# Low parts of later weights by an accumulating load, and a reordered end, in a gated mix of an S4D convolution and a bilinear unit

## The chip, the cores and the metric

The kernel runs on one core of a Trainium2 chip. The metric is the device time of one execution in microseconds. A profile of one execution gives the span from its first to its last instruction and what each engine did: PE (TensorE, matmuls), DVE (VectorE), ACT (ScalarE), POOL (GpSimd) and SP (SyncE, which here only issues DMAs).

## The reference

```python
# u: (1, 2048, 512), N = 128, F = 1792
def _A_ref(u, ...):
    ...
    P = jnp.exp((A * dt[:, None])[:, :, None] * pos[None, None, :])
    K = 2.0 * jnp.einsum("dn,dnl->dl", C, P).real
    ...                                        # y = causal convolution of u with K, by FFT of length 2L
    return y + u * D_skip[None, None, :]

def _B_ref(x, w_gate, w_up, w_down):
    g = jnp.einsum("bsd,df->bsf", x, w_gate)
    u = jnp.einsum("bsd,df->bsf", x, w_up)
    h = g * u
    return jnp.einsum("bsf,fd->bsd", h, w_down)

g = _sigmoid((x * gate_w).sum(-1, keepdims=True))
return g * a + (1 - g) * b                     # a = _A_ref(x, ...), b = _B_ref(x, ...)
```

## The kernel before

**Two computations share the engines.** The bilinear unit is made of dense matmuls. The hidden columns F are 14 tiles of 128, taken in four groups, `GROUPS` = 0 to 2, 3 to 5, 6 to 9 and 10 to 13. For each group the four chunks of 512 tokens are walked, forwards and backwards in turn. For each tile f of the group `hidden` makes two products, pg (gate) and pu (up), 12 matmuls each; ScalarE copies pg out of its bank into h, VectorE multiplies it by pu. pg and pu have one buffer each, so the next pg waits for that copy. `down` then multiplies the group's h with the down weights into y, and `evacuate` scales y by one minus the gate into acc, which GpSimd adds to the output in HBM with an accumulating DMA. For the last group and the last chunk (`LAST` = 0) the rows are kept and added by `ends`.

**High and low parts.** Each operand is held as two numbers of the matmul's format: a high part (the rounded value) and a low part (what the rounding left). A product is three matmuls: high by low, low by high, high by high. The names are whi and wlo (gate and up weights, 1024 columns, halves c = 0 and 1), dhi and dlo (down weights, 512), xs (tokens), hh and hl (h). `weights` and `down_weights` load a weight tile by SP into raw (two buffers) and call `split`, which makes the high part by a ScalarE cast and the low part by a VectorE subtraction:

```python
add("act", 0.62, lambda: act.copy(at(hi, s), src()), r=[got], w=[ph], rank=0)
add(
    "dve", 0.69,
    lambda: dve.tensor_tensor(out=at(lo, z), in0=src(), in1=at(hi, s).bitcast(F32), op=ALU.subtract),
    r=[got, ph], w=[pl], rank=0,
)
```

A low part of gate and up is thus two subtractions, each on its half. `SLOTS` = 4 buffers hold the parts of a group; the next group's weights are made while the last chunk of the old group is worked on. This is called a change of groups below; there are three.

**The convolution** runs beside it on whatever time is left. `u_part` transforms the input (stored as su_d). Sixteen blocks of channels go through `phases`, `amplitudes`, `direct_powers`, `x_table` and `v_table`, which are long chains on ScalarE (exponentials and sines, with table loads between, squares) and VectorE (tiles t, rt, e, ri, su, di, m, x, v), to `k_block`, small matmuls k<-v,x. Four blocks are one quarter q of the channels, transformed in `k_first` (stored as sk_d). `transforms(q)` then makes the product in the frequency domain, T = 0 to 3 (`m_load`, `m_second`, `m_product`), goes back in `m_inverse` (stored as y_d) and in `m_last`, which multiplies by the gate and adds to the output by accumulating DMAs. In the last two quarters the 4 rows of each partition that belong to `ends` are kept (`late["fin"]`); `ends` loads those rows of the output into sums (traced as kt), adds the two kept pieces and acc, and stores them by SP (out<-kt).

**What sets the order.** Nothing above is issued as written. Each step is a task with an engine, a duration in microseconds, what it reads and writes, and a rank. `Work.run` plans all tasks by these numbers and then issues them; `InOrder` keeps each engine to the planned order. So a duration in the text moves instructions, and a change of one task can move any of the others. On the chip each engine takes its queue in order and waits at each instruction for what it needs. Traces show all instructions under line 119, that of `InOrder`; tiles tell them apart.

Of the kernel before, what the change touches and what calls it, by code (L numbers as in the profile page):

```python
# [319 lines left out]
def gated_mix_kernel(  # L320
# [33 lines left out]
    m_su, m_sk, m_y, m_out, m_xs = (work.memory() for _ in range(5))  # L354
# [111 lines left out]
    def weights(fs):  # L466
        for f in fs:
# [113 lines left out]
    def ends():  # L581
# [5 lines left out]
            w=[sums, *((m_out, t0 + r) for r in range(4))], dma=1024, rows=range(t0, t0 + 4),  # L587
        )
        for r, acc in ending:
            t = t0 + r  # L590
            for q, (fin, parts) in late["fin"].items():
                add(
                    "dve", 0.25,
                    lambda r=r, q=q, fin=fin: dve.tensor_tensor(
                        out=sums.t[:, r, P * q : P * q + P], in0=sums.t[:, r, P * q : P * q + P],
                        in1=fin.t[:, 4 * (LAST % 2) + r], op=ALU.add,
                    ),
                    r=parts, w=[(sums, (r, q))], rank=0,
# [47 lines left out]
    def u_part(t):  # L646
# [4 lines left out]
        def score_of(j):  # L651
# [3 lines left out]
                "dve", 0.77,  # L655
# [191 lines left out]
    def phases(b):  # L847
# [3 lines left out]
        tt(0.83, lambda: t.t, lambda: per_power(rates()[:, 1]), lambda: per_channel(turns), ALU.mult, [par, m_powers], [t])  # L851
        add("act", 0.77, lambda: act.activation(rt.t, t.t, AF.Identity, bias=shift[:, 0:1]), r=[t, m_const], w=[rt])

        add(
            "dve", 0.83,
# [6 lines left out]
            "act", 2.13 if b % 2 or not b else 0.83, lambda: act.activation(t.t, t.t, AF.Sin, scale=-TWO_PI), w=[t],  # L862
        )
        add(
            "act", 0.83, lambda: act.activation(rt.t, rt.t, AF.Sin, scale=-TWO_PI, bias=half_pi[:, 0:1]), r=[m_const],
# [6 lines left out]
    def direct_powers(b):  # L872
# [4 lines left out]
        for c in range(2):  # L877
            f = t if c else rt
            tt(0.83, lambda c=c: ri.t[:, c], lambda f=f: f.t, ampl, ALU.mult, [f, e], [(ri, c)])
# [72 lines left out]
    def v_table(b):  # L952
# [8 lines left out]
        add("act", 1.28, copies, r=[ri], w=[(v, 2)])  # L961
# [5 lines left out]
        for to, of, n in (((33, 64, 2), (0, 16, 1), 16), ((34, 64, 4), (33, 49, 2), 8)):  # L967
# [11 lines left out]
            us = 0.04 * n + 0.08  # L979
            add("act", 1.15 if n == 16 else 0.73, sq_act, r=src_parts, w=[(v, ("r", k)), sq])  # L980
# [15 lines left out]
    def k_block(b, x, v):  # L996
# [18 lines left out]
        add("act", 0.4, lambda: act.copy(side(1), pv(0)[:, :, :, ::-1]), r=[pk], w=[(kt, (1, b % 4))])  # L1015
# [398 lines left out]
```

## Time and profile before

| | |
|---|---|
| median of 3 runs | 606.57 us (606.55 to 610.38) |
| profiled execution | 608.69 us, span 606.9 us, granted clock 0.989 |
| PE busy | 586.3 us, 97% |
| DVE busy | 527.0 us, 87% |
| ACT busy | 389.8 us, 64% |
| POOL busy | 113.9 us, 19% |
| DMA moved | 129.73 MB, mean 214 GB/s |

The span leaves out what lies before the first and behind the last instruction. Matmuls overlap one another in the pipeline, so the busy time of PE is near the span even where it runs smoothly; what it loses is read from the starts of its instructions. A row of the timeline gives start, duration, engine, operation, output and inputs, and in brackets how long the engine was idle before it and who released it.

### The profile page before, as it was taken

What the parts mean: (1) busy time and instruction counts of PE and PEld (TensorE: products, weight loads), DVE (VectorE), ACT (ScalarE), POOL (GpSimd) and SP (SyncE); (2) the same over time, 40 slices, a digit from 0 to 9 for tenths busy, and PEclk for the clock granted to TensorE, in tenths of its full rate; (3) what the DMA queues carried; (4) which work ended last, traced back from release to release, by engine and by line L of the source; (5) the groups of instructions that cost most, each with busy time, mean ns of one, the idle gap of its engine ahead of it and who ended that gap; (6) DMA issues with size and microseconds to landing.
All of it is one profiled execution on the core that took longest, in us unless ns stands there. A gap on an engine that the chain in (4) does not pass through costs nothing.

```text
span 606.9 us, 15872 instructions
## 1 busy us (share of the span) xinstructions
PE 586.3 (97%) x6500; PEld 444.8 (73%) x6500; DVE 527.0 (87%) x841; ACT 389.8 (64%) x879; POOL 113.9 (19%) x173
## 2 busy tenths in 40 slices
PE   8889999999999999999999999999899999999993
PEld 5657676787877777786687877866688777777772
DVE  6999999999999999999799999979999950775725
ACT  5279688686679588758958665966877423434621
POOL 0011212300201340201324101003424021402101
PEclk9989999999999999999999999999899999999997
DMA  8899978575647796749989827886989269989876
GB/s 278 313 354 341 360 263 326 161 218 162 136 151 206 211 226 192 161 135 283 237 178 228 185 81 192 198 228 178 204 171 234 63 170 343 207 257 232 214 155 121
DMA packets 69276, 129.73 MB, mean 214 GB/s; under 512 B 6868, under 2 KB 35540, under 8 KB 66772
## 3 DMA queue, kind: packets, MB, share of 16 engines
q1 hardware_dynamic: 47476, 88.21, 45.8%
q0 software_dynamic: 21312, 40.38, 33.1%
q8 instruction: 51, 0.84, 0.6%
q14 instruction: 21, 0.17, 0.1%
q10 hardware_dynamic: 416, 0.13, 0.1%
HBM read 73.65 MB, written 55.05 MB: 212 GB/s over the span
## 4 chain that ended last, share of the span: by engine, by line
PE 67%; DVE 16%; DMA 10%; issue 4%; ACT 2%; POOLq 0%; SPq 0%; ACTq 0%; DVEq 0%; POOL 0%
PE pg L119 19%; PE pu L119 18%; PE y L119 17%; PE k L119 13%; DMA raw<-in_wts 5%; DVE v L119 3%; DVE x L119 2%; DMA y_d<-e 2%; DMA dt_d<-small 2%; DVE wlo L119 1%; DVE y L119 1%; DVE ri L119 1%; DVE t L119 1%; DVE m L119 1%; DMA x<-dt_d 1%
## 5 line engine op out<-in xcount | busy, mean ns | idle before, releaser
L119 PE MATMUL pg<-xs,whi 128*128 128x512 f32 x448 | 140.1, 394 | 0.5 <-ACT whi L119 0.4
L119 PE MATMUL pu<-xs,whi 128*128 128x512 f32 x448 | 138.2, 390 | 0.0
L119 PEld LDWEIGHTS pg<-xs,whi 128*128 128x128 f32 x448 | 85.0, 190 | 19.8 <-ACT whi L119 1.9
L119 PEld LDWEIGHTS pu<-xs,whi 128*128 128x128 f32 x448 | 84.1, 188 | 17.0
L119 PE MATMUL pg<-xs,wlo 128*128 128x512 f32 x224 | 90.2, 403 | 4.3 <-ACT h L119 3.8
L119 PE MATMUL y<-dhi,hl 128*128 128x512 f32 x224 | 91.1, 407 | 2.9 <-ACT acc L119 1.8
L119 PE MATMUL y<-dlo,hh 128*128 128x512 f32 x224 | 88.2, 394 | 1.6 <-DVE dlo L119 1.6
L119 PE MATMUL pu<-xs,wlo 128*128 128x512 f32 x224 | 89.6, 400 | 0.0
L119 PE MATMUL y<-dhi,hh 128*128 128x512 f32 x224 | 87.9, 393 | 0.0
L119 POOL DMA_DIRECT2D out<-acc x44 | 38.7, 918 | 243.3 <-ACT acc L119 204.7
L119 ACT COPY ev<-k 128x512 f32<-128x512 f32 x112 | 59.2, 594 | 17.2 <-PE k L119 17.2
L119 ACT CAST hh<-h 128x512 fp32r<-128x512 f32 x56 | 34.8, 621 | 44.6 <-DVE h L119 44.4
L119 PEld LDWEIGHTS y<-dhi,hl 128*128 128x128 f32 x224 | 42.4, 189 | 24.3 <-issue 7.8
L119 ACT ACTIVATE acc<-y,ngate 128x512 f32<-128x512 f32 x63 | 42.7, 688 | 25.6 <-PE y L119 20.6
L119 PEld LDWEIGHTS pg<-xs,wlo 128*128 128x128 f32 x224 | 42.5, 190 | 21.5 <-ACT h L119 6.8
L119 PEld LDWEIGHTS pu<-xs,wlo 128*128 128x128 f32 x224 | 42.0, 188 | 15.7 <-issue 7.0
L119 ACT COPY h<-pg 128x512 f32<-128x512 f32 x56 | 32.9, 587 | 31.5 <-PE pg L119 26.1
L119 DVE TENSOR_TENSOR h<-pu,h 128x512 f32<-128x512 f32 x56 | 38.6, 689 | 16.6 <-PE pu L119 15.4
L119 PEld LDWEIGHTS y<-dlo,hh 128*128 128x128 f32 x224 | 42.4, 189 | 9.8 <-DVE dlo L119 1.9
L119 PEld LDWEIGHTS y<-dhi,hh 128*128 128x128 f32 x224 | 42.5, 190 | 9.2
L119 DVE TENSOR_TENSOR hl<-h,hh 128x512 fp32r<-128x512 f32 x56 | 38.5, 688 | 3.7 <-ACT hh L119 3.4
L119 POOL DMA_DIRECT2D su_d<-ev x32 | 17.4, 550 | 96.4 <-ACT ev L119 96.4
(124 smaller groups left out, 1004.2 us busy)
## 6 DMA issues: line engine op xcount, KB each, us to landing
xs<-xs_d SPq DMA_DIRECT2D x36, 512.0 KB, 6.0
out<-acc POOLq DMA_DIRECT2D x44, 256.0 KB, 6.4
raw<-in_wts SPq DMA_DIRECT2D x36, 256.0 KB, 3.7
xs_d<-xs SPq DMA_DIRECT2D x16, 512.0 KB, 7.9
su_d<-ev POOLq DMA_DIRECT2D x32, 256.0 KB, 6.1
y_d<-ts SPq DMA_DIRECT2D x14, 512.0 KB, 4.9
in<-su_d POOLq DMA_DIRECT2D x24, 256.0 KB, 7.9
sk_d<-ev SPq DMA_DIRECT2D x6, 1024.0 KB, 5.6
```

The source lines that it names most:

```text
L119: got = getattr(self.engine, name)(*args, **kw)
```

## The change

**Low parts.** For the groups after the first, the gate and up weights (11 tiles of 1024) and, for the second and third group, the down weights (7 tiles of 512) get their low part in another way. ScalarE writes minus the high part into it, and GpSimd issues a DMA that adds the weight itself from HBM to it. VectorE no longer takes part. The raw buffer is read by the ScalarE cast alone. The down weights of the last group still use `split`.

**The end.** `ends` no longer adds pieces that were multiplied by the gate before; the multiplication moves into its addition, and the multiplications of those pieces go. In the last quarters the other piece is handled ahead of the kept one, and the half without it (g = 1) ahead of the half with it. The third quarter's `m_last` may start on PE only behind the last `m_inverse` of the fourth (m_turn), and the load of sums is planned behind the first inverse of the fourth.

**Durations.** Some twenty of the planner's durations are set anew; the diff shows some of them.

```diff
+    def high(hi, c, key):
+        t = raws[key]
+        add("act", 0.62, lambda: act.copy(hi.t[:, c * D : (c + 1) * D], t.t), r=[t], w=[(hi, c)], rank=0)
+
+    def rest(hi, lo, src, n):
+
+        add("act", 0.19 + 0.43 * n, lambda: act.mul(lo.t, hi.t.bitcast(F32), -1.0), r=[hi], w=[lo], rank=0)
+        add("pool", 0.95, lambda: pool_q.dma_start(lo.t, src, accum_op=ALU.add), w=[lo], dma=512 * n, rank=0)
...
                 load(("w", f, c), wts[f][:, c * D : (c + 1) * D])
-                split(ws[f][0], ws[f][1], c, ("w", f, c))
+                if f in GROUPS[0]:
+                    split(*ws[f], c, ("w", f, c))
+                else:
+                    high(ws[f][0], c, ("w", f, c))
+            if f not in GROUPS[0]:
+                rest(*ws[f], wts[f][:, : 2 * D], 2)
...
-            split(wd[f][0], wd[f][1], None, ("w", f, 2))
+            if f in GROUPS[0] or f in GROUPS[-1]:
+                split(*wd[f], None, ("w", f, 2))
+            else:
+                high(wd[f][0], 0, ("w", f, 2))
+                rest(*wd[f], wts[f][:, 2 * D :], 1)
...
             "sp", 0.42, lambda: sp.dma_start(sums.t, ov[:, t0 : t0 + 4, :]),
-            w=[sums, *((m_out, t0 + r) for r in range(4))], dma=1024, rows=range(t0, t0 + 4),
+            r=[(m_y, (KT - 1, 0))], w=[sums, *((m_out, t0 + r) for r in range(4))], dma=1024, rows=range(t0, t0 + 4),
...
-                    lambda r=r, q=q, fin=fin: dve.tensor_tensor(
-                        out=sums.t[:, r, P * q : P * q + P], in0=sums.t[:, r, P * q : P * q + P],
-                        in1=fin.t[:, 4 * (LAST % 2) + r], op=ALU.add,
+                    lambda r=r, q=q, t=t, fin=fin: dve.scalar_tensor_tensor(
+                        sums.t[:, r, P * q : P * q + P], fin.t[:, 4 * (LAST % 2) + r], gate[:, t : t + 1],
+                        sums.t[:, r, P * q : P * q + P], op0=ALU.mult, op1=ALU.add,
                     ),
...
-        add("act", 1.28, copies, r=[ri], w=[(v, 2)])
+        add("act", 1.46, copies, r=[ri], w=[(v, 2)])
...
-            us = 0.04 * n + 0.08
-            add("act", 1.15 if n == 16 else 0.73, sq_act, r=src_parts, w=[(v, ("r", k)), sq])
+            us = 0.69 if n == 16 else 0.63
+            add("act", 1.17 if n == 16 else 0.89, sq_act, r=src_parts, w=[(v, ("r", k)), sq])
...
-        add("pe", 2.13, fn, r=[*ys, *ws], w=banks, rank=1, hold=sts, many=apart_of(q))
+        add("pe", 2.13, fn, r=[*ys, *ws], w=[*banks, (m_turn, (q, T0))], rank=1, hold=sts, many=apart_of(q))
...
-            cuts = ((0, 1), (1, 1)) if q >= KT - 2 and g == LAST // 2 else ((0, 2),)
+            cuts = ((1 - LAST % 2, 1), (LAST % 2, 1)) if q >= KT - 2 and g == LAST // 2 else ((0, 2),)
...
-            "pe", 0.2 + 0.86 * len(gs), fn, r=[*src, m_w4], w=[b for bs in banks for b in bs], rank=1,
+            "pe", 0.2 + 0.86 * len(gs), fn, r=[*src, m_w4, *([(m_turn, (KT - 1, 2))] if q == KT - 2 else [])], w=[b for bs in banks for b in bs], rank=1,
...
-            args = ("dve", 0.15 + 0.54 * n, mix_dve) if q == KT - 1 else ("act", 1.14 * n, mix_act)
-            add(*args, r=[(m_gate, r // 4) for r in range(r0, r0 + 4 * n, 4)], w=parts)
             if n == 1 and n0 == LAST % 2:
                 late.setdefault("fin", {})[q] = t, parts
                 continue
+            args = ("dve", 0.15 + 0.54 * n, mix_dve) if q == KT - 1 else ("act", 1.22 * n, mix_act)
+            add(*args, r=[(m_gate, r // 4) for r in range(r0, r0 + 4 * n, 4)], w=parts)
...
-            for g in range(2):
+            for g in (1 - LAST // 2, LAST // 2):
```

**What moves, at three places.** A number behind a name tells tiles of one name apart. First ScalarE at the first change of groups, around the copy of the old group's first column in its last chunk (pg_1025 before, pg_1027 in the change). Before:

```order
L119 ACTIVATE acc_1220<-y_1195,ngate_84 128x512
L119 COPY x_1228<-pb_485 128x64
L119 ACTIVATE rt_1212<-t_1193 128x672
L119 ACT_TABLE_LOAD
L119 ACTIVATE t_1193<-t_1193 128x672
L119 COPY h_1245<-pg_1025 128x512
L119 ACTIVATE rt_1212<-rt_1212,fixed_82 128x672
L119 CAST whi_1168<-raw_1097 128x512
```

In the change:

```order
L119 ACTIVATE acc_1221<-y_1097,ngate_84 128x512
L119 COPY x_1227<-pb_485 128x64
L119 COPY h_1241<-pg_1027 128x512
L119 CAST whi_1175<-raw_1102 128x512
L119 ACTIVATE wlo_1253<-whi_1175 128x1024
L119 CAST hh_1261<-h_1241 128x512
L119 ACTIVATE rt_1197<-t_1187 128x672
L119 COPY h_1289<-pg_1244 128x512
L119 ACT_TABLE_LOAD
L119 ACTIVATE t_1187<-t_1187 128x672
```

The table load and the sine now stand behind two h copies instead of ahead of the first, and the write of minus the high part (wlo_1253) stands between these copies.

Then GpSimd's queue at the same change: the last stores of the transformed input, the first loads of it, and what follows. Before:

```order
L119 DMA su_d_57<-ev_1279 128x512 x4
L119 DMA in_1348<-su_d_57 64x8x128 x2
L119 DMA in_1373<-su_d_57 64x8x128 x2
L119 DMA out_0<-acc_1830 128x512
L119 DMA out_0<-acc_1839 128x512
```

In the change:

```order
L119 DMA wlo_1253<-in_wts 128x1024
L119 DMA su_d_57<-ev_1301 128x512 x4
L119 DMA wlo_1366<-in_wts 128x1024
L119 DMA in_1458<-su_d_57 64x8x128 x2
L119 DMA in_1482<-su_d_57 64x8x128 x2
L119 DMA wlo_1523<-in_wts 128x1024
L119 DMA dlo_1613<-in_wts 128x512
L119 DMA dlo_1632<-in_wts 128x512
L119 DMA dlo_1696<-in_wts 128x512
L119 DMA wlo_1830<-in_wts 128x1024
L119 DMA out_0<-acc_1856 128x512
```

Seven accumulating loads enter the queue between the stores and the first accumulating stores of the output: those of columns 3, 4 and 5, of their down weights, and of column 6.

Last the end on VectorE; x holds the fourth quarter's pieces, kt the rows of `ends`. Before:

```order
L119 TENSOR_TENSOR kt_6444<-kt_6444,x_7304 128x128 x2
L119 TENSOR_TENSOR kt_6444<-acc_7500,kt_6444 128x512
L119 TENSOR_TENSOR kt_6444<-acc_7502,kt_6444 128x512
L119 TENSOR_TENSOR kt_6444<-kt_6444,x_7304 128x128 x2
L119 TENSOR_TENSOR kt_6444<-acc_7554,kt_6444 128x512
L119 TENSOR_TENSOR x_7383<-k_7521,x_7383 128x2x256 x2
L119 TENSOR_TENSOR x_7383<-x_7383,gate_83 128x1024
L119 TENSOR_TENSOR kt_6444<-raw_7574,kt_6444 128x512
```

In the change:

```order
L119 TENSOR_TENSOR x_7301<-k_7491,x_7301 128x2x256 x2
L119 TENSOR_TENSOR x_7301<-x_7301,gate_83 128x1024
L119 TENSOR_TENSOR x_7299<-k_7505,x_7299 128x256 x4
L119 TENSOR_TENSOR x_7299<-x_7299,gate_83 128x512
L119 SCALAR_TENSOR_TENSOR kt_7222<-x_7299,gate_83,kt_7222 128x128 x2
L119 TENSOR_TENSOR kt_7222<-acc_7529,kt_7222 128x512
L119 TENSOR_TENSOR kt_7222<-acc_7534,kt_7222 128x512
L119 SCALAR_TENSOR_TENSOR kt_7222<-x_7299,gate_83,kt_7222 128x128 x2
L119 TENSOR_TENSOR kt_7222<-acc_7563,kt_7222 128x512
L119 TENSOR_TENSOR kt_7222<-raw_7578,kt_7222 128x512
```

The whole piece of 1024 columns, which stood between the last two additions, is now worked first, and the four rows end the queue.

More of the change, by code (lines that the diff above doesn't have):

```diff
@@ L353, in gated_mix_kernel @@
     xs_d = dram.tile([4, KT, P, 2, D], F32, name="xs_d")
-    m_su, m_sk, m_y, m_out, m_xs = (work.memory() for _ in range(5))
+    m_su, m_sk, m_y, m_out, m_xs, m_turn = (work.memory() for _ in range(6))
     pools = {n: open_pool(n, b, PSUM) for n, b in (("ps_y", 2), ("ps_g", 1), ("ps_k", 4))}
@@ L654, in score_of @@
             add(
-                "dve", 0.77,
+                "dve", 0.73,
                 lambda: dve.scalar_tensor_tensor(
@@ L861, in phases @@
         add(
-            "act", 2.13 if b % 2 or not b else 0.83, lambda: act.activation(t.t, t.t, AF.Sin, scale=-TWO_PI), w=[t],
+            "act", 2.07 if b % 2 or not b else 0.77, lambda: act.activation(t.t, t.t, AF.Sin, scale=-TWO_PI), w=[t],
         )
         add(
-            "act", 0.83, lambda: act.activation(rt.t, rt.t, AF.Sin, scale=-TWO_PI, bias=half_pi[:, 0:1]), r=[m_const],
+            "act", 0.85, lambda: act.activation(rt.t, rt.t, AF.Sin, scale=-TWO_PI, bias=half_pi[:, 0:1]), r=[m_const],
             w=[rt],
@@ L1014, in k_block @@
         side = lambda h: kt.t[:, h, :, g0 : g0 + 8].rearrange("p b g k -> p g b k")
-        add("act", 0.4, lambda: act.copy(side(1), pv(0)[:, :, :, ::-1]), r=[pk], w=[(kt, (1, b % 4))])
+        add("act", 0.37, lambda: act.copy(side(1), pv(0)[:, :, :, ::-1]), r=[pk], w=[(kt, (1, b % 4))])
         for h, op in enumerate((ALU.add, ALU.subtract)):
             add(
-                "dve", 0.4, lambda h=h, op=op: dve.tensor_tensor(out=side(h), in0=pv(1), in1=side(1), op=op),
+                "dve", 0.42, lambda h=h, op=op: dve.tensor_tensor(out=side(h), in0=pv(1), in1=side(1), op=op),
                 r=[pk, (kt, (1, b % 4))], w=[(kt, (h, b % 4))], rank=0,
@@ L1073, in evict @@
         if q == KT - 1 and n % 2:
-            add("dve", us, lambda: dve.tensor_copy(to(), src()), r=r, w=w)
+            add("dve", us + 0.1, lambda: dve.tensor_copy(to(), src()), r=r, w=w)
         else:
@@ L1102, in m_load @@
                 add(
-                    "pool", 1.2,
+                    "pool", 0.88,
                     lambda w=w, src=src, p=p, r0=r0: pool_q.dma_start(
```

10 lines of the change are left out of this document (5 added, 5 removed).

## The prediction

> **What bounds the kernel now.** The page first: who is busy, and what the chain that ended last is made of.
>
> ```profile
> span 606.9 us, 15872 instructions
> PE 586.3 (97%) x6500; PEld 444.8 (73%) x6500; DVE 527.0 (87%) x841; ACT 389.8 (64%) x879; POOL 113.9 (19%) x173
> PE 67%; DVE 16%; DMA 10%; issue 4%; ACT 2%; POOLq 0%; SPq 0%; ACTq 0%; DVEq 0%; POOL 0%
> ```
>
> TensorE is the bound. The matmuls overlap, so their own lengths say little; the chain in order of time gives the pace: twelve matmuls of the gated unit in 2.72 us, a K block of small ones in 2.05.
>
> ```profile
> 110.60 2.72 PE pu L119 x12
> ...
> 168.19 2.05 PE k L119 x125
> ```
>
> Both kernels issue the same matmuls, so only what TensorE loses can be won. In windows of 20 us (PE is the first pair) nearly every one from 80 to 580 reads like this:
>
> ```profile
> 120.00:140.00 20.00, 20.00 (x208) 16.53 (x207) 19.88 (x33) 17.10 (x47) 0.00 (x0) 1.00 0.69 182
> ```
>
> The timeline of TensorE shows the two gaps that stand out, around 104 and 430; the time behind the last matmul is the third loss.
>
> ```profile
> 104.13 0.61 PE L119 MATMUL pu<-xs,whi 128*128 128x512 f32 x2
> 106.31 0.50 PE L119 MATMUL pg<-xs,wlo 128*128 128x512 f32 x1 [1.57 <-ACT h L119]
> ...
> 430.05 0.61 PE L119 MATMUL pu<-xs,whi 128*128 128x512 f32 x2
> 432.68 0.50 PE L119 MATMUL pg<-xs,wlo 128*128 128x512 f32 x1 [2.02 <-ACT h L119]
> 433.02 0.95 PE L119 MATMUL pg<-xs,whi 128*128 128x512 f32 x2
> ...
> 437.11 0.39 PE L119 MATMUL pu<-xs,wlo 128*128 128x512 f32 x1
> ...
> 597.07 0.39 PE L119 MATMUL y<-dhi,hh 128*128 128x512 f32 x1
> ```
>
> Two matmuls take 0.45 of the 2.18 from 104.13 to 106.31: 1.7 us lost. At 430 it is 2.63 less 0.45, so 2.2, and then twelve starts from 432.68 to 437.11 take 4.43 instead of 2.72 at a lower clock: 1.7 more, 3.9 in all. Both wait for the ScalarE copy h, since pg has one buffer. What held h there:
>
> ```profile
> 103.73 1.28 ACT L119 ACT_TABLE_LOAD   x1
> 105.02 0.76 ACT L119 ACTIVATE t<-t 128x672 f32<-128x672 f32 x1
> 105.69 0.57 ACT L119 COPY h<-pg 128x512 f32<-128x512 f32 x1
> ...
> 431.52 0.62 ACT L119 CAST dhi<-raw 128x512 fp32r<-128x512 f32 x1 [0.65 <-DMA raw<-in_wts]
> 432.05 0.58 ACT L119 COPY h<-pg 128x512 f32<-128x512 f32 x1
> ```
>
> At 104 a table load and a sine stand ahead of h; at 430 a cast that waits for a late weight load does. And the end:
>
> ```profile
> 596.22 1.41 DVE L119 TENSOR_TENSOR x<-k,x 128x512 f32<-128x512 f32 x2
> 597.66 1.23 DVE L119 TENSOR_TENSOR x<-x,gate 128x1024 f32<-128x1024 f32 x1
> 598.80 0.68 DVE L119 TENSOR_TENSOR kt<-raw,kt 128x512 f32<-128x512 f32 x1
> ...
> 597.49 0.69 ACT L119 ACTIVATE raw<-y,ngate 128x512 f32<-128x512 f32 x1 [2.03 <-PE y L119]
> ...
> 599.31 1.54 POOL L119 DMA_DIRECT2D out<-x  x1 [3.91 <-DMA out<-kt]
> ...
> SPq L1408 <- DMA out<-x: 4.1, 1, 4.1
> ```
>
> The last store that anybody waits for is not the last rows (out<-kt) but the 512 KB accumulating store out<-x: SyncE's final wait is 4.1 us longer for it. (The page puts the 3.91 down to out<-kt; the multiply that feeds the store ended at 598.89, and I read that as the true releaser.)
>
> **The change, part by part.** *The swap of engines.* The groups of instructions and the DMA table price what goes and the nearest rows to what comes.
>
> ```profile
> L119 DVE TENSOR_TENSOR wlo<-raw,whi 128x512 fp32r<-128x512 f32 x22 | 14.5, 687 | 4.1 <-ACT whi L119 4.1
> L119 DVE TENSOR_TENSOR dlo<-raw,dhi 128x512 fp32r<-128x512 f32 x14 | 9.6, 685 | 1.0 <-ACT dhi L119 0.8
> L119 ACT CAST whi<-raw 128x512 fp32r<-128x512 f32 x22 | 13.3, 621 | 4.9 <-DMA raw<-in_wts 4.5 <-PE pu L119 0.4
> L119 ACT ACTIVATE rt<-t 128x672 f32<-128x672 f32 x16 | 12.3, 772 | 13.9 <-DVE t L119 13.9
> ...
> L119 POOL DMA_DIRECT2D out<-acc x44 | 38.7, 918 | 243.3 <-ACT acc L119 204.7
> ...
> out<-acc POOLq DMA_DIRECT2D x44, 256.0 KB, 6.4
> ...
> out<-ts POOLq DMA_DIRECT2D x4, 512.0 KB, 7.3
> ...
> out<-in POOLq DMA_DIRECT2D x1, 512.0 KB, 10.8
> ...
> out<-x POOLq DMA_DIRECT2D x1, 512.0 KB, 6.5
> ```
>
> VectorE loses 22 x 0.687 = 15.1 us and 7 of the 14 dlo subtractions, 4.8: 19.9 together. ScalarE gains eleven writes of minus the high part over 1024 elements. No row has that; 672 elements take 0.77 and two casts of 512 take 1.24, and the slope from 512 to 672 (0.151/160) gives 1.10, which I take. With seven of 512 at 0.62 that is 12.1 + 4.3 = 16.4 us on a ScalarE that is 64% busy. GpSimd issues 18 more DMAs of some 0.9 us, idle 80% of the time: nothing. None of this lies on TensorE's path by itself: 0. Its cover is ScalarE's idle time, and what it costs without that is the second rival.
>
> *The wait that is new.* The products with a low part now wait for a DMA to land. Nothing in the trace accumulates into on-chip memory; the nearest rows are the accumulating stores above, 6.4 us for 256 KB and 6.5 to 10.8 for 512 KB, and I take these as the bounds, the low end as likelier because a low part has 2 or 4 KB to a row and these stores have 512 bytes. Against that stands what TensorE has to do meanwhile. At the second and third change of groups the new columns have 20 us and more, because a slot comes free when the last token chunk has used it and three or four columns and all their down products follow. The first change is the tight one. Between the writes stand squares and a rounding, as here:
>
> ```profile
> 407.92 0.86 ACT L119 ACTIVATE rt<-rt,fixed 128x672 f32<-128x672 f32 x1
> 408.68 0.66 ACT L119 ACTIVATE v<-v 128x512 f32<-128x512 f32 x1
> 409.22 0.62 ACT L119 ACTIVATE sq<-v 128x512 f32<-128x512 f32 x1
> ...
> 410.90 0.68 ACT L119 ACTIVATE v<-v 128x256 f32<-128x256 f32 x1
> 411.38 0.42 ACT L119 ACTIVATE sq<-v 128x256 f32<-128x256 f32 x1
> ```
>
> The write for the third down weight (dlo_1696) ends some 6.2 us after the second new column's pg is complete: h 0.59, two pairs of squares 1.3 and 1.1, rt 0.86, and hh, dhi and the write at 0.62 each, with half a us of waiting. TensorE meanwhile has 52 matmuls at 0.227 and a K block of 2.05, 13.8 us. That leaves 7.6 for the landing: 1.2 to spare by the 256 KB row. The third column (wlo_1523) has 66 matmuls, 15.0, less 2.0 on ScalarE: 13 against at most 10.8. Cost: 0, up to 5 at the top of the bounds. Behind this wait stand TensorE's next columns, so its whole queue would stand still.
>
> *The gap at 430.* Raw buffers are now freed by the cast alone, not by the subtraction.
>
> ```profile
> SPq L119 <- DVE wlo L119: 43.9, 18, 8.2
> ```
>
> SyncE waited 43.9 us for these subtractions before it could load the next weight. With that wait gone the load that held the cast at 431.52 starts earlier, so I take the gap as closed: -3.9 (between 0 and -3.9).
>
> *The gap at 104.* In the new order h stands ahead of the table load and the sine. It can start as pg ends, near 104.0, instead of 105.69; its 0.59 remains, so 1.3 of the 1.7 go: -1.3 (0 to -1.7).
>
> *The end.* The 512 KB store is now made first and the last rows last. Its matmuls precede the last one by 45 of 0.227 and the other eight-matmul pair, some 10 us; copies, adds (1.4), multiply (1.23), issue (1.54) and 6.5 us of landing end before the last rows are stored. The closing waits fall to those for out<-kt: -4.1. The last addition can also start 0.6 sooner, since raw was ready at 598.2 and the multiply held it: bounds -2 to -4.7. It needs y_d written in time: the last inverse now comes 8.9 us of matmuls earlier than before, so its transfers are covered.
>
> *The rebuilt order.* The new durations move rows everywhere. Before has two gaps of this kind in some 500 us. I allow for one new one at the dearer price, +3.9. Where I would look: ScalarE at the third change, where a table load, 21 exponentials, four copies and an rt stand between two h copies.
>
> One rule of the Trainium skill speaks against the price of these gaps: TensorE: Matmul & The Clock Gate, section HAM oscillation, says that the clock holds unless TensorE is idle for more than some 3.4 us. By it a gap of 2.0 costs 2.2, and closing the one at 430 and opening another still cancel; the trace disagrees (2.02 us idle, then 1.7 us lost to slow starts).
>
> **Sum.** -4.1 - 3.9 - 1.3 + 3.9 = -5.4 us on the profiled span of 606.9: 601.5. That execution took 608.69 with what lies around the span, where the median of the three runs is 606.57; I take the difference from the median: 601.2.
>
> **Rivals.** *No new gap* (0.20): all terms without the allowance and the 0.6: 606.57 - 9.9 = 596.7. For it: TensorE's queue is already full for 500 us; against it: an h copy has only the 2.72 of the pu product less its own 0.59, 2.1 us, of slack, and there are 56.
>
> *ScalarE becomes the bound at the changes of groups, slower* (0.11). Place: the h copies beside the eleven writes.
>
> ```profile
> 100.00:140.00 40.00, 38.43 (x298) 30.53 (x298) 38.70 (x59) 31.41 (x71) 4.92 (x9) 1.00 0.66 206
> ```
>
> ScalarE (fourth pair) is busy 31.41 of 40 us at the first change; four writes and three small ones add 6.3, 37.7. From 40 on it decides, and its in-order waits for VectorE (13.9 us for t over the run) can use up the 2.3 left. If every write is exposed and the two gaps stay: -4.1 + 12.1, 614.6. Against it: VectorE, which it waits for, is relieved in the same stretch.
>
> *The low parts land late* (0.12): accumulating into on-chip memory at twice the 6.4 of the store, 12.8, is 5.2 over the 7.6, and a gap of that length brings the slow clock, 1.9: 601.2 + 7.1 = 608.3. The Trainium skill, DMA: Bandwidth & Descriptors, section Anatomy of one DMA, fits 2.0 us plus bytes by 436 GB/s; an estimate from it for 512 KB is 3.2, and by that this rival would vanish; the rows here are two to three times as long.
>
> *The gaps only move* (0.12): the tail is won, the two old gaps stay in other places and one comes: -4.1 + 3.9, 606.4.
>
> **How the numbers follow.** The forecast has 0.45, with its own range of 598.5 to 604.5. The range from 596 to 610 holds it, the late landing, the moved gaps and most of the first rival. 1% is 6.1 us, about what a measurement of this kernel can tell from no change: below 600.5 lie the first rival and a third of the forecast, 0.35; above 612.6 most of the ScalarE case, 0.10; the rest, 0.55.
>
> **What would show it.** Right: the final wait for out<-x gone and the program ending on out<-kt; no idle of TensorE near 104 and 430 with h as releaser; the first product with a low part after each change of groups without a wait on a DMA; VectorE busy near 507 us, ScalarE near 406. Wrong: idle of TensorE put down to wlo or dlo at the first change, ScalarE full there, or the last accumulating store still last.

## The result and the profile after

The changed kernel takes 602.92 us (median of 5 runs, 601.78 to 603.81), the kernel before on the same chip 607.08 (median of 5). The ratio is 0.9926, with a 95% interval of 0.9901 to 0.9950: faster by 0.7%, within the range that was called no change. The forecast was 601.2. The profiled execution of the changed kernel took 601.78 us, with a span of 600.0 against 606.9; of these 6.9 us some 2.7 are scatter, since the one profiled before lay 1.6 above its median and this one 1.1 below.

The page first, as before: who is busy, and what the chain that ended last is made of.

```profile
span 600.0 us, 15878 instructions
PE 585.8 (98%) x6500; PEld 443.4 (74%) x6500; DVE 512.3 (85%) x811; ACT 401.0 (67%) x893; POOL 128.9 (21%) x191
PE 79%; DVE 8%; ACT 6%; DMA 5%; issue 1%; ACTq 0%; DVEq 0%
```

TensorE has 79% of the chain instead of 67. On its timeline the places of the two old gaps, and then the longest idle times that are left between 46 and 590 us:

```profile
104.11 0.61 PE L119 MATMUL pu<-xs,whi 128*128 128x512 f32 x2
104.73 0.50 PE L119 MATMUL pg<-xs,wlo 128*128 128x512 f32 x1
...
405.31 0.50 PE L119 MATMUL pu<-xs,wlo 128*128 128x512 f32 x1 [0.43 <-DVE h L119]
...
419.88 0.50 PE L119 MATMUL y<-dhi,hl 128*128 128x512 f32 x1 [0.39 <-ACT acc L119]
...
560.50 0.50 PE L119 MATMUL pu<-xs,wlo 128*128 128x512 f32 x1 [0.50 <-issue]
...
593.95 0.39 PE L119 MATMUL y<-dhi,hh 128*128 128x512 f32 x1
```

The pg product at 104.73 follows the pu pair without a wait on h, nothing stands at 430, and no idle time is over 0.50. On ScalarE, h now stands ahead of the table load and starts as pg ends:

```profile
104.09 0.59 ACT L119 COPY h<-pg 128x512 f32<-128x512 f32 x1 [1.87 <-PE pg L119]
...
108.88 1.28 ACT L119 ACT_TABLE_LOAD   x1
```

The end, on GpSimd, on VectorE, and SyncE's closing wait:

```profile
588.21 1.54 POOL L119 DMA_DIRECT2D out<-x  x1 [16.12 <-DVE x L119]
...
595.10 0.69 DVE L119 TENSOR_TENSOR kt<-raw,kt 128x512 f32<-128x512 f32 x1 [2.02 <-ACT raw L119]
...
SPq L1426 <- DMA out<-kt: 2.4, 1, 2.4
```

The accumulating store out<-x is issued 11 us earlier, nobody waits for it any more, and the program ends on the last rows. From the start of the last product to the end of the span it was 606.9 - 597.07 = 9.8 us and is 600.0 - 593.95 = 6.0.

The groups and DMA issues of the part that was swapped, and two of SyncE's waits for raw buffers:

```profile
L119 ACT ACTIVATE wlo<-whi 128x1024 fp32r<-128x1024 f32 x11 | 11.7, 1062 | 0.1
L119 ACT ACTIVATE dlo<-dhi 128x512 fp32r<-128x512 f32 x7 | 4.4, 633 | 0.0
...
wlo<-in_wts POOLq DMA_DIRECT2D x11, 512.0 KB, 7.3
...
dlo<-in_wts POOLq DMA_DIRECT2D x7, 256.0 KB, 5.9
...
SPq L119 <- ACT whi L119: 29.7, 14, 5.8
SPq L119 <- DMA raw<-in_wts: 28.5, 13, 7.9
```

Of the 43.9 us that SyncE waited for the subtractions of gate and up 0.7 are left (of those of the down weights, 15.7 of 20.6, since the last group still uses them); it waits for casts now, and for raw loads, which land in 5.2 us (the median) instead of 3.7.

### The profile page after: what moved, and what is told of

Its sections match the earlier page's. It is cut to its first block, busy times and chain, and to the rows that moved or that the text cites. A ratio compares the mean times of both kernels' runs of the same rounds, so it can differ in the third digit from the quotient of the medians.

```text
span 600.0 us, 15878 instructions
## 1 busy us (share of the span) xinstructions
PE 585.8 (98%) x6500; PEld 443.4 (74%) x6500; DVE 512.3 (85%) x811; ACT 401.0 (67%) x893; POOL 128.9 (21%) x191
## 2 busy tenths in 40 slices
DMA packets 71867, 137.33 MB, mean 229 GB/s; under 512 B 7156, under 2 KB 35828, under 8 KB 69364
## 3 DMA queue, kind: packets, MB, share of 16 engines
q1 hardware_dynamic: 47476, 88.21, 45.9%
## 4 chain that ended last, share of the span: by engine, by line
PE 79%; DVE 8%; ACT 6%; DMA 5%; issue 1%; ACTq 0%; DVEq 0%
PE y L119 22%; PE pu L119 21%; PE pg L119 21%; PE k L119 15%; DMA raw<-in_wts 4%; DVE x L119 2%; DVE y L119 1%; DVE v L119 1%; ACT ts L119 1%; ACT whi L119 1%; DMA y<-in_xT 1%; ACT L119 1%; DVE h L119 1%; DVE t L119 1%; DVE xs L119 1%
## 5 line engine op out<-in xcount | busy, mean ns | idle before, releaser
L119 ACT COPY ev<-k 128x512 f32<-128x512 f32 x112 | 59.2, 595 | 15.7 <-PE k L119 15.6
L119 ACT COPY h<-pg 128x512 f32<-128x512 f32 x56 | 33.1, 590 | 29.7 <-PE pg L119 27.8
```

Source lines behind the costliest of these rows:

```text
L119: got = getattr(self.engine, name)(*args, **kw)
```

## The experiments

**Theory and rival.** My theory after the result was the prediction's: the gap at 430 closed because the cast alone frees a raw buffer, the end gained by its own edits, and the swap costs nothing. The rival was that the rebuilt order did it all. Four kernels took the change apart.

*Old order, new mechanism.* The planner sees the old tasks; only what the second subtraction of a weight issues is replaced.

```diff
-            lambda: dve.tensor_tensor(out=at(lo, z), in0=src(), in1=at(hi, s).bitcast(F32), op=ALU.subtract),
+            late or (lambda: dve.tensor_tensor(out=at(lo, z), ...)),
...
+    def rest(hi, lo, src):
+        act.mul(lo.t, hi.t.bitcast(F32), -1.0)
+        pool_q.dma_start(lo.t, src, accum_op=ALU.add)
...
+                late = (lambda: None) if c == 0 else (lambda f=f: rest(*ws[f], wts[f][:, : 2 * D]))
```

> The order of the kernel before is kept on every engine (the planner sees the old tasks and the old durations); alone the low parts of the later groups are now minus the high part, written by ScalarE where the subtraction stood, plus an accumulating load. Durations and the end are those of before. My theory: the gap of 3.9 us near 430 came from raw buffers that the subtraction on VectorE freed late, so it closes even in the old order: 606.6 - 3.9 = 602.7, SyncE's wait for wlo (43.9 us) is gone, and no idle of TensorE near 430. Rival, the order does it: the gaps are closed by where h stands in the new order, so this one keeps both gaps and reads 606 to 608. Rival, the wait is not free: the write stands ahead of an h copy or a low part lands late in an order not made for it, 608 or more.

Measured: ratio 1.0166 (1.0135 to 1.0196), span 615.4, 8.5 longer. My theory missed by 15 us of median (617.5 for 602.7). The last rival's number held, but hardly its reason: no product waits for a low part, and of the writes one, 0.62 us long, stands ahead of the h copy that was late. A new gap of 4 us stood near 134, on TensorE and on ScalarE:

```profile
137.91 0.79 PE L119 MATMUL pg<-xs,wlo 128*128 128x512 f32 x1 [4.01 <-ACT h L119]
...
134.91 0.69 ACT L119 ACTIVATE acc<-y,ngate 128x512 f32<-128x512 f32 x1 [4.43 <-DMA out<-acc]
```

ScalarE waited for a plain store of SyncE to land (those of the first group are not accumulating), and the cast and h behind it in its queue waited with it. With the half clock that went with it (136 to 143 us), this place cost most of the 8.5 us. A second gap of 2.71 us, for hl from VectorE, stands at 422.75, and of the old gap at 430 0.79 is left, at 441.98. The stretch from 110 to 140 us tells why. First the windows of the kernel before, of this one and of the changed kernel (last three columns: clock, DMA share, GB/s), then the landing of out<-acc there in the same three:

```profile
110.00:140.00 30.00, 30.00 (x252) 24.80 (x251) 29.65 (x45) 23.16 (x58) 4.91 (x8) 1.00 0.64 183
...
110.00:140.00 30.00, 25.99 (x229) 21.16 (x228) 22.61 (x34) 22.20 (x56) 8.60 (x13) 0.94 0.94 234
...
110.00:140.00 30.00, 29.57 (x247) 23.83 (x246) 27.69 (x41) 28.50 (x66) 8.49 (x12) 1.00 0.90 221
```

```profile
out<-acc SPq DMA_DIRECT2D x4, 256.0 KB, 2.2
...
out<-acc SPq DMA_DIRECT2D x4, 256.0 KB, 8.5
...
out<-acc SPq DMA_DIRECT2D x4, 256.0 KB, 9.5
```

The accumulating loads fill the DMA engines (0.64 to 0.94), and stores that landed in 2.2 us take 8.5. In the changed kernel the engines are as full and the same stores land later still, in 9.5 us, but TensorE is busy for 29.57 of the 30 us: there ScalarE does not wait for any of them. So late landing costs time only where the order has no room for it.

*New order, old mechanism.* In the changed kernel's order the subtraction is issued right behind the cast.

```diff
             act.copy(hi.t[:, cs], t.t)
+            dve.tensor_tensor(out=lo.t[:, cs], in0=t.t, in1=hi.t[:, cs].bitcast(F32), op=ALU.subtract)
...
-        add("pool", 0.95, lambda: pool_q.dma_start(lo.t, src, accum_op=ALU.add), w=[lo], dma=512 * n, rank=0)
+        add("pool", 0.95, lambda: None, w=[lo], dma=512 * n, rank=0)
```

> The order of the changed kernel is kept on every engine, its end and its durations too; alone the low parts of the later groups are again formed by the subtraction on VectorE, issued right behind the cast, without minus the high part and without accumulating loads. My theory: VectorE gets 20 us of work back and the raw buffers are freed by the subtraction again, so the loads are late and a gap of 2 to 4 us comes back at a change of groups: 605 to 607. Rival, the order does it: the tail and both gaps stay closed, 602 to 604. In both the end stays as in the changed kernel (last wait of SyncE on out<-kt, 2.4 us).

Measured: ratio 1.0253 (1.0234 to 1.0272), span 622.6; both were far off. On TensorE the waits name VectorE, or nothing that the profile shows (issue):

```profile
116.81 0.79 PE L119 MATMUL pu<-xs,wlo 128*128 128x512 f32 x1 [2.01 <-DVE h L119]
149.21 1.00 PE L119 MATMUL k<-v,x 128*32 128x64 f32 x55 [1.46 <-DVE v L119]
...
475.61 0.80 PE L119 MATMUL y<-dhi,hl 128*128 128x512 f32 x1 [4.11 <-issue]
```

So neither order carries the gain by itself: the mechanism loses 8.5 us in the old order, and the new order loses 22.6 without the mechanism. Each was run in an order that was not planned for it.

*The end alone.* The kernel before with the edits of `ends`, `m_turn`, `m_last` and `transforms` only:

```diff
-            cuts = ((0, 1), (1, 1)) if q >= KT - 2 and g == LAST // 2 else ((0, 2),)
+            cuts = ((1 - LAST % 2, 1), (LAST % 2, 1)) if q >= KT - 2 and g == LAST // 2 else ((0, 2),)
...
-            for g in range(2):
+            for g in (1 - LAST // 2, LAST // 2):
```

> The kernel before with the edits of the end alone (last sums by one multiply and add, the last stores in the other order, the last inverse ahead, the load of the sums held back); old split, old durations, so the order differs only from the last part of the program on. My theory: the time behind the last product falls by 3.8 us, as the two traces show, and the gaps near 104 and 430 stay: 602.8. Rival: the end gains only beside the rebuilt order, because the last stores then have other work in front, and this one reads 605 to 608.

Measured: ratio 1.0023 (1.0009 to 1.0038), span 607.1: nothing gained. The gap near 430 is there as before, but without the slow starts behind it (more on this below). The closing wait is on out<-kt alone, as in the changed kernel, and yet it is 607.1 - 595.99 = 11.1 us from the start of the last product to the end:

```profile
432.68 0.50 PE L119 MATMUL pg<-xs,wlo 128*128 128x512 f32 x1 [2.12 <-ACT h L119]
...
SPq L1408 <- DMA out<-kt: 3.6, 1, 3.6
```

What counts is the last transform back, the small matmuls k<-x,w_t of `m_last` in the fourth quarter, which feed those sums (some of the expectations call it the last inverse; it is not the `m_inverse` of the prediction's 8.9 us). It has 18 matmuls of the down product behind it here, 33 in the changed kernel, so VectorE does its sums after the last matmul instead of beside it. The rival held.

*The low parts alone*, planned anew, with the old durations and the old end:

```diff
-            split(wd[f][0], wd[f][1], None, ("w", f, 2))
+            if f in GROUPS[0] or f in GROUPS[-1]:
+                split(*wd[f], None, ("w", f, 2))
+            else:
+                high(wd[f][0], 0, ("w", f, 2))
+                rest(*wd[f], wts[f][:, 2 * D :], 1)
```

> The kernel before with the low parts by accumulating load alone, planned anew with the old durations and the old end (the planner counts the writes and the loads with their own durations). My theory: the gap near 430 closes, the old end stays (final wait on out<-x, some 4 us): 606.6 - 3.9 = 602.7, 601 to 604. Rival, the order does it: any rebuilt order draws its gaps anew, so 603 to 610 with gaps in other places, h named as the releaser.

Measured: ratio 1.0071 (1.0048 to 1.0093), span 610.4. The rival held in the main, 0.4 over its range, with gaps in new places, some of which name a transfer and not h; two of them, then the window around the first and the landing there (315 to 345 us):

```profile
339.55 2.33 PE L119 MATMUL k<-in,w2s 32*32 32x256 f32 x60 [1.41 <-DMA in<-sk_d]
...
442.07 0.50 PE L119 MATMUL pg<-xs,wlo 128*128 128x512 f32 x1 [1.63 <-ACT h L119]
...
320.00:345.00 25.00, 20.98 (x192) 14.75 (x192) 19.07 (x27) 13.24 (x22) 9.81 (x13) 0.86 1.03 213
...
in<-sk_d POOLq DMA_DIRECT2D x5, 256.0 KB, 11.8
```

The DMA engines are full here too, the input of k<-in,w2s lands in 11.8 us (7.1 is the median of the whole run), and TensorE works 20.98 of 25 us. The end, 5.2 us, is shorter than the changed kernel's although it is the old one: 57 matmuls of the bilinear unit stand behind the last transform back.

**New theory.** The three parts have no price of their own; VectorE's relief lets the planner put the last transform back further ahead, and the traced durations keep that plan from breaking. The planner's own end of each plan gave the numbers for the other four combinations' expectations. The durations alone:

```diff
-        add("act", 1.28, copies, r=[ri], w=[(v, 2)])
+        add("act", 1.46, copies, r=[ri], w=[(v, 2)])
```

> The kernel before with the traced durations in the planner alone: old split on VectorE, old end. Theory now: the end is set by where the last inverse stands among the last down products, and the planner can only bring it forward when VectorE is relieved; with the longer durations and the subtractions still on VectorE its own plan ends at 600.3 instead of 591.9 (it plans a gap of 3.7 us ahead of the last products), so the span is near 612, slower than before. Rival, the durations carry the gain: a plan with true durations has no gaps, whatever is planned, so 598 to 602 on the span.

Measured: ratio 1.0198 (1.0159 to 1.0236), span 620.2. Slower as the theory said, by 8 us more. The last transform back stands behind all products, and the program still waits for out<-x:

```profile
601.04 0.39 PE L119 MATMUL y<-dhi,hh 128*128 128x512 f32 x1
601.36 3.79 PE L119 MATMUL k<-x,w_t 64*32 64x512 f32 x32
...
SPq L1408 <- DMA out<-x: 5.1, 1, 5.1
```

The change without the end edits:

```diff
-            for g in (1 - LAST // 2, LAST // 2):
+            for g in range(2):
```

> The changed kernel with the old end (the low parts by accumulating load and the traced durations stay). Theory now: low parts and durations together close the gaps, and the plan ends at 590.3, 2.0 later than that of the changed kernel: span near 602, losses of TensorE between 46 and 560 us near those of the changed kernel. Rival, the end edits are worth the 3.8 us by themselves: 604 or more, ending on the wait for out<-x.

Measured: ratio 0.9982 (0.9961 to 1.0003), span 605.6: the rival held, in number and in the wait at the end. TensorE loses 2.28 us in one place near 550, and at 151.74 a product waits 1.01 us for a low part (DMA dlo<-in_wts), the only such wait in an order with single loads. The closing wait is on out<-x:

```profile
550.02 1.16 PE L119 MATMUL k<-y,w3s 32*64 32x128 f32 x30 [2.28 <-issue]
...
SPq L1426 <- DMA out<-x: 3.7, 1, 3.7
```

So the end edits are worth 5.6 us of span (3.4 by the ratios, 0.9982 to 0.9926) on top of the other two parts, and nothing by themselves. The change with the subtraction back, planned anew:

```diff
-                if f in GROUPS[0]:
-                    split(*ws[f], c, ("w", f, c))
-                else:
-                    high(ws[f][0], c, ("w", f, c))
+                split(ws[f][0], ws[f][1], c, ("w", f, c))
```

(and the same for the down weights).

> The changed kernel with the old subtraction on VectorE, planned anew (end edits and traced durations stay). Theory now: VectorE is the engine that the end waits for; the plan ends at 595.2, 6.9 later than that of the changed kernel, so the span is 606 to 609. Rival, the low parts are worth nothing by themselves and only reorder: 600 to 602.

Measured: ratio 1.0067 (1.0028 to 1.0106), span 611.9, three over the theory's range and far from the rival's. And the change with the old durations:

```diff
-        add("act", 1.46, copies, r=[ri], w=[(v, 2)])
+        add("act", 1.28, copies, r=[ri], w=[(v, 2)])
```

> The changed kernel with the old durations in the planner (low parts by accumulating load and the end edits stay). Theory now: the plan is the most hopeful of all (586.5) but with durations that are too short it does not hold: gaps at the changes of groups as with the low parts alone, span 607 to 612. Rival, the durations are only bookkeeping: 600 to 603.

Measured: ratio 1.0072 (1.0042 to 1.0102), span 613.7. That is 1.7 over the theory's range, but this was the longest of eight executions; the median, 612.31 with some 1.8 outside the span, lies inside. As with the low parts alone, the gaps of late transfers come back, the longest of them

```profile
438.89 2.17 PE L119 MATMUL k<-in,w_t 64*32 64x512 f32 x14 [3.00 <-DMA in<-y_d]
```

All combinations, with the ratio to the kernel before, the span, the start of TensorE's last matmul, the time from there to the end of the span, and the matmuls of the bilinear unit behind the last transform back (those over 48 are of gate and up, the others of the down product). Each span is of one execution; those of one kernel differ by up to 8 us, so small differences are read from the ratios.

| kernel | ratio | span | last matmul | time to the end | matmuls behind the transform |
|---|---|---|---|---|---|
| before | 1 | 606.9 | 597.07 | 9.8 | 21 |
| low parts | 1.0071 | 610.4 | 605.17 | 5.2 | 57 |
| end | 1.0023 | 607.1 | 595.99 | 11.1 | 18 |
| durations | 1.0198 | 620.2 | 604.56 | 15.6 | 0 |
| low parts, end | 1.0072 | 613.7 | 608.47 | 5.2 | 75 |
| low parts, durations | 0.9982 | 605.6 | 596.58 | 9.0 | 24 |
| end, durations | 1.0067 | 611.9 | 600.72 | 11.2 | 9 |
| all three (the change) | 0.9926 | 600.0 | 593.95 | 6.0 | 33 |

The three parts alone add up to 2.9% slower; together they are 0.7% faster. The time behind the last matmul follows the number of matmuls behind the last transform back, with either end: 15.6 with none, 9 to 11 with 9 to 24, 6.0 with 33, and 5.2 from 57 on. The reason can be read from the start of that transform's own last matmul: from there to the end it is 13.7 to 15.6 us in all six kernels with up to 33 (15.0 before, 591.87 to 606.9; 14.3 in the change, 585.63 to 600.0). That tail hardly changes; what changes is how much of it TensorE's remaining work covers. With 57 and more, the last rows alone decide, at 5.2.

**What the traffic costs.** The run in the old order again, with the write but without the load; its low parts stay minus the high part.

```diff
         act.mul(lo.t, hi.t.bitcast(F32), -1.0)
-        pool_q.dma_start(lo.t, src, accum_op=ALU.add)
```

> The run in the old order with minus the high part written by ScalarE, but without the accumulating loads: the low parts stay minus the high part (so the products with them are other numbers), and 7.4 MB of transfers are gone. In the old order with the loads TensorE stood still for 4.0 us near 134, because h stood behind a gate multiply that waited 4.4 us for a store out<-acc to land; the stores landed in 8.5 us there instead of 2.2, with the DMA engines full. Theory: the traffic does it, so without the loads that wait goes and the stores land in 2 to 4 us again: span 607 to 611 instead of 615.4. Rival: the writes on ScalarE do it, at places that the old order did not make for them: 613 to 617, with the gap near 134 still there.

Measured: ratio 0.9970 (0.9947 to 0.9992), span 602.9: 12.5 us less than with the loads (11.9 by the ratios), more than the theory asked for. The wait near 134 is gone (1.12 us for h is left at 141.00) and out<-acc lands in 2.7 us between 110 and 140. And the gap at 430 is closed in the old order: there the cast of dhi and h follow each other without a wait.

```profile
out<-acc SPq DMA_DIRECT2D x4, 256.0 KB, 2.7
...
428.91 0.61 ACT L119 CAST dhi<-raw 128x512 fp32r<-128x512 f32 x1
429.42 0.58 ACT L119 COPY h<-pg 128x512 f32<-128x512 f32 x1
```

So the relief of VectorE and the freed raw buffers are worth 606.9 - 602.9 = 4.0 us between these two executions, with the writes already on ScalarE; 1.7 of that are the slow starts at 430, which not every execution has. By the ratio it is 1.8 (0.5 to 3.2). The loads take back some 12 there.

*Twice the writes*, in the changed kernel's own order:

```diff
-        add("act", 0.19 + 0.43 * n, lambda: act.mul(lo.t, hi.t.bitcast(F32), -1.0), r=[hi], w=[lo], rank=0)
+        add("act", 0.19 + 0.43 * n, lambda: [act.mul(...) for _ in range(2)], r=[hi], w=[lo], rank=0)
```

> The changed kernel in its own order, with minus the high part written twice each time: 16 us more of ScalarE, nothing else. Theory: the writes lie under other work, except that the third down weight of the first change has only half a us to spare (7.33 us from the issue of its load to its first product, of which 0.86 are the issue and 5.9 the landing): 0 to 3 us more, 603 to 606. Rival: ScalarE is the bound at the changes of groups: 10 us more or over, 612 and up.

Measured: ratio 1.0028 (1.0015 to 1.0042), span 606.9: 6.9 us more (6.2 by the ratios) for 14.6 us of ScalarE (415.6 busy instead of 401.0), between the two expectations, and not where I had said. No product waits for a low part; what is late stands behind the writes on ScalarE, at the first and the third change:

```profile
123.68 0.50 PE L119 MATMUL y<-dhi,hl 128*128 128x512 f32 x1 [1.21 <-DVE hl L119]
409.85 0.50 PE L119 MATMUL pu<-xs,wlo 128*128 128x512 f32 x1 [1.51 <-DVE h L119]
426.60 0.50 PE L119 MATMUL y<-dhi,hl 128*128 128x512 f32 x1 [1.58 <-ACT acc L119]
```

*Twice the loads:*

```diff
+            for _ in range(2):
+                pool_q.dma_start(lo.t, src, accum_op=ALU.add)
```

> The changed kernel in its own order, with each accumulating load done twice onto minus twice the high part (the low part comes out doubled), so that each lands some 7 us later and moves twice the bytes. Theory: only the first change has no room: the third down weight comes 6 us late, the third column 4, the second 2; these are shared, so 5 to 10 us more, 608 to 613, with TensorE's waits on dlo and wlo there and none at the later changes, which have 17 to 29 us from issue to product. Rival: the full DMA engines cost more than the lateness, because stores and loads of others land late: over 613, with waits on other transfers at the later changes too.

Measured: ratio 1.1078 (1.1054 to 1.1102), span 671.2, 71 us more. TensorE waits for the low parts themselves, seven times, 41 us in all, and at every change of groups (136 to 176, 320 to 334 and 513 us), where the theory had such waits at the first alone:

```profile
PE y L119 <- DMA dlo<-in_wts: 20.7, 4, 10.8
PE pg L119 <- DMA wlo<-in_wts: 20.4, 3, 9.7
```

A single load landed about as fast as before (medians 6.6 and 6.9 us for the columns and the down weights), but GpSimd waits for the first to land before it issues the second onto the same tile, so everything behind it in GpSimd's queue is late, the next low parts and the stores out<-acc. ScalarE waits for one of these stores, and h behind it, which is another 9.8 us of TensorE. GpSimd's own waits, and ScalarE:

```profile
POOL wlo L119 <- DMA wlo<-in_wts: 86.2, 10, 13.5
POOL dlo L119 <- DMA dlo<-in_wts: 37.8, 5, 10.1
...
291.42 0.69 ACT L119 ACTIVATE acc<-y,ngate 128x512 f32<-128x512 f32 x1 [11.25 <-DMA out<-acc]
```

The number is the rival's, its cause is so for that one wait only. The edit made the low parts later not by the second landing alone but also by what GpSimd's queue then held up, so how late a low part alone may be stays open.

*A try at a better version:* the down weights of the second group by subtraction again.

```diff
-            if f in GROUPS[0] or f in GROUPS[-1]:
+            if f in GROUPS[0] or f in GROUPS[1] or f in GROUPS[-1]:
```

> The changed kernel, planned anew with the down weights of the second group by subtraction on VectorE again (the condition takes in that group): this takes three accumulating loads, and the one that has half a us to spare, out of the stretch in which the DMA engines are full. The plan ends 1.9 us earlier than that of the changed kernel. Theory: 1 to 3 us faster than the changed kernel, 600 to 602. Rival: any new order draws its gaps anew, 604 to 610.

Measured: ratio 1.0030 (1.0015 to 1.0046), span 605.6. The rival held: the time behind the last matmul is down to 5.2, and TensorE loses more than that in small waits, such as

```profile
274.73 0.50 PE L119 MATMUL pg<-xs,wlo 128*128 128x512 f32 x1 [1.64 <-ACT kt L119]
```

The planner's own end was 1.9 us better than the changed kernel's, so that end does not rank orders this close. No run beat the change.

## Why the prediction was right, and where it was not

*The end, -4.1:* the size was right (9.8 to 6.0, so -3.8), the cause only half. I put it to the store of 512 KB being made first. The same edits alone shortened nothing. What the time follows is how many matmuls stand behind the last transform back, 21 before and 33 after: the twelve more cover 3.1 us of a tail that itself became only 0.7 shorter (15.0 to 14.3). I had counted the matmuls behind this transform in the change, and the 8.9 us by which the last `m_inverse` comes earlier, and used both only as cover for the stores and transfers.

*The gap at 430, -3.9:* right that it closes, and the reason is shown: it closes in the old order as soon as the subtractions are off the raw buffers. The price was that of one execution. Behind a gap of 2.02 us the clock in the kernel before fell to half for 3.4 us, which is the 1.7 of slow starts; behind the same gap, 2.12 us, in the run with the end alone it did not fall. The same window in both, with the clock third from the end:

```profile
432.00:438.00 6.00, 5.32 (x16) 4.28 (x17) 5.55 (x9) 5.66 (x15) 3.15 (x4) 0.72 1.16 196
...
432.00:438.00 6.00, 5.32 (x73) 4.08 (x82) 5.54 (x9) 5.55 (x15) 2.98 (x4) 1.00 1.16 197
```

So 1.7 of the 3.9 need not be in a median that the profiled execution lay 1.6 above. The forecast came out 1.7 too low (601.2 for 602.92), which may be this or chance. The 1.9 of slow clock in the rival of the late landing has no row either.

*The gap at 104, -1.3:* right in place and reason; h precedes the table load, and the wait of 1.57 us is gone. That it needs the new order fits the old-order runs, which keep a wait of about 1 us there (0.95 and 0.97).

*One new gap, +3.9:* not one but a little in several places. The last matmul starts 3.1 us earlier where the two gaps promised 5.2, so 2.1 came back, most of it in waits of half a us and less, which grew from 0.9 to 2.5 us. In the other seven orders that were planned anew the gaps were there, and dearer; spans ran from 605.6 to 620.2. An allowance was the right thing; that of the eight the given one was the best is not something the profile of before could tell.

*The swap, 0:* the reasoning failed here, though the total did not show it. I counted ScalarE's 16.4 us (11.7 + 4.4 measured), GpSimd's issues and the landing of the low parts themselves (6.4 assumed for 256 KB, 5.9 measured; no product waited for one), and left out the 16 DMA engines that every other transfer shares. The row for 100 to 140 that I quoted had their share, 0.66, in its column beside the clock. With 7.6 MB more (137.33 for 129.73), stores and raw loads elsewhere land late: some 12 us in an order not made for it. The Trainium skill says as much in DMA: Bandwidth & Descriptors, section Issuing engines are not separate DMA queues: transfers started by any engine run on the same 16 DMA engines and interleave. The traces agree: loads on GpSimd's queue moved stores on SyncE's from 2.2 to 8.5 us. In the changed kernel's own order the price can hardly be more than the 2.5 us of idle time that are left to TensorE after the first 46 us, but no run leaves out the loads in that order. That 0 was near enough there is owed to an order with room for late transfers, for which I had not argued; in that it was luck. Nor is ScalarE's share free: a second dose of writes cost 0.47 us for each us (6.9 for 14.6).

*Busy times:* VectorE near 507 was forecast, 512.3 came; ScalarE 406, 401.0 came. The groups are as priced (the 22 wlo and 7 dlo subtractions are gone), but the busy time counts overlapping instructions once, and neighbours on an engine overlap, so the sum of a group's durations overstates what its busy time loses or gains. In the old order, where only these 29 subtractions go, VectorE lost 15.9 us (527.0 to 511.1) for a sum of 19.9.

*The rivals.* "The gaps only move" and "ScalarE becomes the bound" describe the kernels around the change better than the change: the low parts alone are the first (610.4 against its 606.4), the doubled writes lean to the second. The late landing named the wrong transfers: with single loads one product in one order waited for a low part (1.01 us), and the rest of what came late was beside them.

*What stays open:* why only the combination of all three holds. Late transfers explain the low parts with the old durations; why the traced durations cost 13 us of span without the low parts is explained by the end (15.6 instead of 9.8) for less than half. Nor is it shown why the order of the change has room for late transfers where the other orders with these loads have not.

## What to carry to other kernels

Work that was handed to the DMA engines delayed the other transfers of that stretch here: read the DMA share there by windows, and ask which store or load would hold an in-order engine if it landed four times later, as the stores here did. Where a planner redraws the order, the parts of a change have no prices that add; price a mechanism with the order held still, and the whole only as a whole. At the end of a program, count how much of the bounding engine's work is left behind the last piece with a long tail.

## What was unexpected of the hardware

The accumulating loads took more DMA time for a megabyte than SyncE's plain transfers, but little more than what GpSimd's queue carried before. The queues of the changed kernel:

```profile
q1 hardware_dynamic: 47476, 88.21, 45.9%
q0 software_dynamic: 23904, 47.98, 40.4%
```

Before, the second read 40.38 MB and 33.1%. The difference is (0.404 x 600.0 - 0.331 x 606.9) / 7.6 = 5.5 us of all 16 engines for a megabyte; q1 has 0.459 x 600.0 / 88.21 = 3.1. But the second queue had 0.331 x 606.9 / 40.38 = 5.0 before, with plain stores, loads and accumulating stores together, so no run here shows how much of the 5.5 is the accumulating and how much the queue. Part of it is also time that the packets share with others, since the engines were fuller. An accumulating load onto on-chip memory landed in 7.3 us for 512 KB and 5.9 for 256; the estimate from the Trainium skill, DMA: Bandwidth & Descriptors, section Anatomy of one DMA, that the prediction gave was 3.2 for the first, and the trace does not agree (its loads ran beside other transfers).

The granted clock is the other point. Leaving out the run with twice the loads, every idle time of TensorE over 2.2 us between 46 and 590 us (2.28, 2.44, 2.71 twice, 3.00, 4.01 and 4.11) went with a stretch at half clock, of 3.4 or 6.8 us. Of the three between 2.0 and 2.2 two did (2.01 and 2.02) and one did not (2.12), and of those near 1.6 some did (1.56 and 1.65 with the durations alone) and others did not (1.57 in the kernel before). So a gap of about 2 us has no fixed price here.
